# A re-ordered start for an RWKV and gated-MLP kernel: outer products later, half-width down projections earlier, idle matmuls moved

## The chip, the cores and the metric

The program runs on one core of a Trainium2 chip. The metric is the device time of the execution in microseconds; three runs of the kernel before gave 528.74, 527.22 and 528.25 us, median 528.25. The profiled execution took 528.38 us, of which its instructions span 526.6.

## The reference

An RWKV recurrence and then a gated feed-forward layer. For each of 4 batches and 8 heads, over 768 tokens with head size 48 and a state of 48 x 48:

```python
for t in range(S):
    kt, vt, rt = (k[:, :, t], v[:, :, t], r[:, :, t])
    cur = np.einsum('bhd,bhe->bhde', u[None] * kt, vt)
    y[:, :, t] = np.einsum('bhd,bhde->bhe', rt, state + cur)
    state = w[None, :, :, None] * state + np.einsum('bhd,bhe->bhde', kt, vt)
...
x = attn_out.transpose(0, 2, 1, 3).reshape(B * S, H * D)      # 3072 x 384
gate = 1.0 / (1.0 + np.exp(-(x @ w_gate)))                    # 384 x 1536
val = x @ w_val
out = gate * val @ w_out                                      # 1536 x 384
```

All inputs and the output are float32.

## The kernel before, in words

The recurrence is cut into 12 chunks of 64 tokens. A chunk has two groups of heads, so there are 24 groups, numbered in the order (chunk 0, g 1), (chunk 0, g 0), (chunk 1, g 1) and so on. A group's work is: load its channels (`L`) and tokens (`X`); scale queries, keys, bonus keys and token keys by tables of decay powers (`R`, `k`, `A`, `T`); 64 small matmuls for the scores (`Z`, line 392); masked copies of the scores out of PSUM by VectorE (`K`, line 400); the outputs (`I`), which are 32 matmuls from the state, a drain and 32 matmuls from the scores, into two banks of PSUM (line 354); 32 matmuls of outer products for the state (`O`, line 354 too), which go into columns 256 to 447 of the same two banks (for group 1 alone into two banks of their own); decay of the state (`d`) and its update (`s`); and x in two float32r parts, a rounded high part (`h`, ScalarE, line 493) and the low rest (`l`, VectorE, line 497). A fill (`F`) moves leftover rows of x by DMA.

The feed-forward layer works on tiles of two chunks (512 columns) and 12 blocks of 128 hidden units. A block has a gate projection (`u`) and a value projection (`v`) of nine matmuls each (line 531; three parts of x times three pairings of high and low parts: the first two matmuls of a part read the high x, the third the low x), a sigmoid (`g`), a product (`m`), the split of h in a high and a low part (`H`, and `q` on POOL or `qv` on VectorE), and nine down-projection matmuls into three accumulators (`D`, line 573). In the first tile, blocks 0 and 1 are computed in two halves of 256 columns, marked a (chunk 0) and b (chunk 1), since the a half can start before chunk 1 is done. Weights come in as raw words (`W`), from which each block's high and low parts are made by a cast (`c`), a join of words (`j`), a rounding (`w`) and a subtraction (`o`).

`N.k` is k matmuls of bf16 128x512 on a constant, whose result nobody reads (`idle_matmuls`, line 641).

PSUM has a ring of three banks (`one_bank`) for the outputs of groups and the projections, two banks for the scores, and three for the accumulators. A new tile of the ring waits until the readers of the old one are done.

The order of the work up to the end of the first tile is written by hand in the string `START`. Each word is a step and its argument: `u.0b` is the gate projection of block 0, half b. Every engine and SP's DMA queue execute their instructions in the order in which the steps stand there; waits between engines come from what the steps read and write, in that same order. After `START` a loop goes over the blocks of the remaining tiles.

```python
for step in START.split():
    name, _, arg = step.partition(".")
    if name == "D":
        finish(block(arg))
    elif name in moe_steps:
        moe_steps[name](moe_of(block(arg)), block(arg)[2])
    else:
        steps[name](*([int(arg)] if arg else []))
```

Of the kernel before, what the change touches and what calls it, by code (L numbers as in the profile page):

```python
# [19 lines left out]
B, H, S, D = 4, 8, 768, 48  # L20
# [22 lines left out]
START = """  # L43
ta L.0 tov.0 tc tb W.0 ts.0 L.1 ts.1 X.0 tz W.1 tk L.2 X.1 to.1 ti.1 X.2 ti.0 A.0 R.0 W.2 k.0 c0.0
tp tr Z.0 tt A.1 K.0 c0.1 tn k.1 I.0 Rv.1 j0.1 h.0 l.0 Tv.0 Z.1 c.1 j0.0 O.0 A.2 j.1 w0.0 sa.0 N.5
T.2 K.1 F.0 w.1 W.3 Rv.2 I.1 T.1 N.4 k.2 L.3 o0v.0 h.1 L.4 Z.2 w0.1 W.4 O.1 X.3 l.1 o0.1 s.1 u.0a
g.0a K.2 v.0a o.1 m.0a c.2 I.2 O.2 R.3 d.2 j.2 u.1a A.3 N.3 H.0a g.1a k.3 h.2 q.0a s.2 v.1a w.2 l.2
m.1a Z.3 T.3 A.4 H.1a N.4 R.4 K.3 c.3 k.4 I.3 O.3 F.2 L.5 W.8 o.2 D.0a X.4 h.3 L.6 Z.4 W.5 l.3 d.3
W.6 L.7 s.3 X.5 u.0b X.6 g.0b j.3 v.0b c.4 w.3 u.2 j.4 qv.1a m.0b H.0b g.2 v.2 q.0b K.4 w.4 Rv.5
u.1b T.4 A.5 v.1b g.1b m.1b D.0b k.5 H.1b I.4 ov.3 O.4 m.2 A.6 R.6 q.1b Z.5 k.6 L.8 d.4 D.1a W.7 h.4  # L50
o.4 s.4 H.2 D.1b K.5 c.6 l.4 Tv.5 u.3 c.5 g.3 j.6 v.3 j.5 qv.2 I.5 h.5 Z.6 l.5 R.7 L.9 A.7 m.3 X.8
d.5 D.2 ub K.6 H.3 O.5 k.7 s.5 w.5 q.3 u.4 c.8 T.6 ov.5 c.7 g.4 v.4 j.7 w.6 m.4 u.5 ov.6 g.5 v.5 I.6
Y.8 R.8 Z.7 W.9 d.6 O.6 W.10 X.7 w.7 W.11 H.4 s.6 X.9 D.3 j.8 h.6 qv.4 w.8 l.6 D.4 m.5 H.5 F.6 ov.7
qv.5 u.6 c.9 g.6 K.7 v.6 ov.8 m.6 Tv.7 H.6 u.7 qv.6 g.7 k.8 v.7 j.9 m.7 w.9 D.5 o.9 u.8 g.8 H.7 v.8
q.7 c.10 D.6 j.10 m.8 I.7 H.8 Z.8 O.7 d.7 R.9 h.7 w.10 s.7 D.7 b.8 ov.10 u.9 l.7 qv.8 g.9 c.11 v.9
F.7 Y.9 j.11 m.9 D.8 w.11 ov.11 u.10 g.10 H.9 qv.9 v.10 m.10 H.10 u.11 qv.10 g.11 t.8 i.8 v.11 K.8
k.9 m.11 D.9 H.11 t.9 D.10 q.11 b.9 T.9 i.9 T.8
"""


# [869 lines left out]
```

## Time and profile before

| | |
|---|---|
| median of 3 runs | 528.25 us |
| profiled execution, time and span | 528.38 us, 526.6 us |
| PE busy (matmul) | 509.7 us, 5220 matmuls |
| DVE, ACT, POOL busy | 202.6, 186.1, 187.2 us |
| largest part of the chain that ended last | up projections (line 531), 56% |
| mean granted TensorE clock | 0.995 of 2.4 GHz |

PE is TensorE's matmuls and PEld its weight loads, which run beside them. DVE is VectorE, ACT ScalarE, POOL GpSimd, SP the queue that issues the DMAs. All times are from the start of the span. The region that the change touches lies between 22 and 60 us.

### The profile page before, as it was taken

To read this page: it belongs to the slowest core of one execution; us is meant where nothing else is said; L and a number is where in the kernel's file an instruction comes from. 1 tells how busy PE (TensorE), PEld (TensorE's weight loads), DVE (VectorE), ACT (ScalarE), POOL (GpSimd) and SP (SyncE) were. 2 spreads that over 40 slices of the span, in tenths; PEclk is the share of its full clock that TensorE was granted. 3 is DMA by queue.
4 is the path that set the end of the run, shared out by engine and by line. 5 is a ranking of instruction groups with operands and counts; after the bars stand their busy time and mean duration, and the time that the engine had idled before them with its cause. 6 is when DMAs were issued, how large, how long until landed. Compare 5 with 4: busy or idle time off the path is not lost.

```text
span 526.6 us, 11976 instructions
## 1 busy us (share of the span) xinstructions
PE 509.7 (97%) x5220; PEld 421.4 (80%) x5220; DVE 202.6 (38%) x345; ACT 186.1 (35%) x395; POOL 187.2 (36%) x158
## 2 busy tenths in 40 slices
PE   3899999999999999999999999999999999999995
PEld 3689788888888788888888888888888888888884
DVE  7877865545242243242341432431442211111112
ACT  5587864534223134233133332331431221311211
POOL 4454402214545252453452452552352111111120
PEclk9899999999999999999999999999999999999999
DMA  8949654123213030420230420312400000100001
GB/s 318 368 144 421 262 191 167 34 75 96 76 64 88 10 107 4 145 88 19 78 98 12 148 87 1 97 36 72 147 17 2 11 7 14 61 0 1 0 2 65
DMA packets 15579, 47.84 MB, mean 91 GB/s; under 512 B 2368, under 2 KB 4928, under 8 KB 14112
## 3 DMA queue, kind: packets, MB, share of 16 engines
q1 hardware_dynamic: 15376, 46.74, 25.5%
q8 instruction: 43, 0.70, 0.6%
q10 hardware_dynamic: 144, 0.26, 0.1%
q14 instruction: 16, 0.13, 0.1%
HBM read 39.92 MB, written 4.72 MB: 85 GB/s over the span
## 4 chain that ended last, share of the span: by engine, by line
PE 95%; DVE 2%; DMA 1%; issue 1%; ACT 0%; SPq 0%; DVEq 0%; ACTq 0%
PE ring L531 56%; PE acc L573 29%; PE ring L354 7%; PE sc L392 3%; DMA chan<-in_ch 1%; DVE score L400 1%; DVE wf L256 0%; PE acc L641 0%; DVE chan L320 0%; ACT dec L296 0%; DVE sg L586 0%; DVE dec L309 0%; DVE xt L497 0%; DVE toks L324 0%; PE acc L354 0%
## 5 line engine op out<-in xcount | busy, mean ns | idle before, releaser
L531 PE MATMUL ring<-xt,wx 128*128 128x512 f32 (+1 forms) x1332 | 306.5, 384 | 0.0
L531 PEld LDWEIGHTS ring<-xt,wx 128*128 128x128 f32 x1332 | 245.2, 188 | 49.8 <-ACT sg L544 0.3
L557 POOL TENSOR_TENSOR h<-sg,h 128x512 fp32r<-128x512 f32 (+1 forms) x65 | 87.1, 1340 | 252.4 <-ACT h L553 252.4
L573 PE MATMUL acc<-h,wx 128*128 128x512 f32 (+1 forms) x666 | 161.3, 387 | 0.0
L573 PEld LDWEIGHTS acc<-h,wx 128*128 128x128 f32 x666 | 121.2, 188 | 25.0 <-DVE h L557 0.2
L548 DVE TENSOR_TENSOR sg<-ring,sg 128x512 f32<-128x512 f32 (+1 forms) x74 | 50.0, 676 | 235.0 <-PE ring L531 233.5
L544 ACT ACTIVATE sg<-ring 128x512 f32<-128x512 f32 (+1 forms) x74 | 43.2, 584 | 156.3 <-PE ring L531 156.3
L553 ACT CAST h<-sg 128x512 fp32r<-128x512 f32 (+1 forms) x74 | 45.0, 609 | 144.1 <-DVE sg L548 137.8
L309 POOL TENSOR_TENSOR dec<-chan,tabk 128x512 f32<-128x512 f32 x21 | 27.7, 1319 | 14.3 <-PE ring L354 14.0
L497 DVE TENSOR_TENSOR xt<-ring,xt 112x256 fp32r<-112x256 f32 (+1 forms) x52 | 19.9, 418 | 32.6 <-ACT xt L493 32.6
L324 POOL TENSOR_TENSOR toks<-toks,tabn 128x384 f32<-128x384 f32 x19 | 23.7, 1253 | 12.5 <-ACT wx L264 9.5
L330 POOL TENSOR_TENSOR dec<-dec,toks 128x384 f32<-128x384 f32 x16 | 16.3, 1017 | 26.9 <-DMA dec<-in_rt 26.7
L320 DVE TENSOR_TENSOR chan<-chan,tabk 128x512 f32<-128x512 f32 x24 | 24.8, 1034 | 0.6 <-ACT dec L296 0.6
L392 PE MATMUL sc<-dec,chan 48*64 48x64 f32 x768 | 17.2, 231 | 7.7 <-DVE chan L320 7.6
L400 DVE COPY_PREDICATED score<-masks,sc 128x512 f32<-128x512 int32 x32 | 23.9, 748 | 1.9 <-PE sc L392 1.1
L447 ACT ACTIVATE state<-state,pw 112x96 f32<-112x96 f32 x80 | 23.4, 362 | 1.8 <-PE ring L354 1.8
L392 PEld LDWEIGHTS sc<-dec,chan 48*64 48x64 f32 x768 | 14.8, 145 | 8.9 <-POOL dec L309 7.6
L466 DVE TENSOR_TENSOR state<-state,ring 48x192 f32<-48x192 f32 (+1 forms) x52 | 17.9, 350 | 8.1 <-PE ring L354 4.3
L256 DVE SCALAR_TENSOR_TENSOR wf<-wr,top 128x1152 int32<-128x1152 int32 (+1 forms) x13 | 16.8, 1304 | 9.5 <-ACT top L249 6.0
L354 PE MATMUL ring<-score,toks 64*48 64x64 f32 (+1 forms) x768 | 16.6, 223 | 3.7 <-issue 2.3
L493 ACT CAST xt<-ring 112x256 fp32r<-112x256 f32 (+1 forms) x52 | 16.7, 363 | 6.6 <-PE ring L354 6.4
L267 POOL TENSOR_TENSOR wx<-wf,wx 128x1152 fp32r<-128x1152 f32 (+1 forms) x5 | 12.5, 2507 | 18.3 <-ACT wx L264 18.3
(63 smaller groups left out, 254.7 us busy)
## 6 DMA issues: line engine op xcount, KB each, us to landing
wr<-in_wt SPq DMA_DIRECT2D x11, 1152.0 KB, 9.1
chan<-in_ch SPq DMA_DIRECT2D x24, 512.0 KB, 4.3
toks<-in_tk SPq DMA_DIRECT2D x24, 400.0 KB, 4.9
out_y<-wf SPq DMA_DIRECT2D x16, 256.0 KB, 2.3
dec<-in_rt SPq DMA_DIRECT2D x16, 192.0 KB, 2.9
xt<-xt SPq DMA_DIRECT2D x30, 64.0 KB, 2.3
wr<-in_wt SPq DMA_DIRECT2D x2, 576.0 KB, 5.5
xt<-xt SPq DMA_DIRECT2D x12, 32.0 KB, 4.3
```

Source lines behind the costliest of these rows:

```text
L309: eng.tensor_tensor(v4(t[:, 0]), v4(chan[n][:, 0]), bc2(table_of(n)[:, :, ::-1]), ALU.mult)
L320: eng.tensor_tensor(v4(k), v4(k), bc2(table_of(n)), ALU.mult)
L324: eng.tensor_tensor(v4(k), v4(k), bc2(tabn[:, 4 * g : 4 * g + 4]), ALU.mult)
L354: nc.tensor.matmul(to[bank][64 * half : 64 * half + m, cs], lhsT, rhs, start=first, stop=stop, skip_group_check=True,)
L392: nc.tensor.matmul(sc[64 * gm : 64 * gm + 64, be, o : o + C], kk[row, cs : cs + C], rr[row, cs : cs + C], start=True, stop=True,)
L400: nc.vector.copy_predicated(t.rearrange("q (b m i) -> q b m i", b=2, m=4), masks[:, m].bitcast(I32).unsqueeze(1).unsqueeze(1).broadcast_to ...
L531: nc.tensor.matmul(o[:, self.cols], w[a][:, g * DM + kt * P : g * DM + (kt + 1) * P], self.x[:, kt, b, self.cols], start=(k == 0), stop=(k ...
L544: nc.scalar.activation(sg[:, c], self.pair[f][0][:, c], AF.Sigmoid, scale=UP)
L548: nc.vector.tensor_tensor(sg[:, c], self.pair.pop(f)[1][:, c], sg[:, c], ALU.mult)
L553: nc.scalar.copy(out=h[:, 0, c], in_=sg[:, c])
L557: eng.tensor_tensor(h[:, 1, c], self.sg.pop(f)[:, c], h[:, 0, c], ALU.subtract)
L573: nc.tensor.matmul(self.acc[d][:, self.cols], w[a][:, 2 * DM + d * P : 2 * DM + (d + 1) * P], h[:, b, self.cols], start=(f == 0 and k == 0 ...
```

## The change

Only the string `START` changes. Seen by engine, the order changes as follows; everything not named keeps its place.

- PE: `N.4` behind `Z.3` is removed and `N.3` is added behind `v.1a`. `O.2 u.1a N.3 v.1a Z.3 N.4 I.3 O.3 D.0a Z.4 u.0b` becomes `O.2 u.1a N.3 v.1a N.3 Z.3 D.0a I.3 Z.4 D.1a O.3 u.0b`, and `Z.5 D.1a D.1b u.3` becomes `Z.5 D.1b u.3`.
- DVE: `s.2 l.2` becomes `l.2 s.2`; the low part of h of block 1a moves to POOL (`qv.1a` becomes `q.1a`).
- ACT: `d.2 A.3 H.0a g.1a h.2 w.2` becomes `A.3 H.0a h.2 g.1a d.2 w.2`; `c.3 h.3 d.3 g.0b c.4` becomes `h.3 d.3 g.0b c.3 c.4`.
- POOL: `q.0a T.3 R.4 o.2` becomes `q.0a R.4 T.3 q.1a o.2`.
- SP: `L.3 L.4 W.4 X.3` becomes `L.3 X.3 L.4 W.4`.

Between engines, `h.3` now stands before `O.3` in the string and `l.3` still behind it.

```diff
-T.2 K.1 F.0 w.1 W.3 Rv.2 I.1 T.1 N.4 k.2 L.3 o0v.0 h.1 L.4 Z.2 w0.1 W.4 O.1 X.3 l.1 o0.1 s.1 u.0a
-g.0a K.2 v.0a o.1 m.0a c.2 I.2 O.2 R.3 d.2 j.2 u.1a A.3 N.3 H.0a g.1a k.3 h.2 q.0a s.2 v.1a w.2 l.2
-m.1a Z.3 T.3 A.4 H.1a N.4 R.4 K.3 c.3 k.4 I.3 O.3 F.2 L.5 W.8 o.2 D.0a X.4 h.3 L.6 Z.4 W.5 l.3 d.3
-W.6 L.7 s.3 X.5 u.0b X.6 g.0b j.3 v.0b c.4 w.3 u.2 j.4 qv.1a m.0b H.0b g.2 v.2 q.0b K.4 w.4 Rv.5
-u.1b T.4 A.5 v.1b g.1b m.1b D.0b k.5 H.1b I.4 ov.3 O.4 m.2 A.6 R.6 q.1b Z.5 k.6 L.8 d.4 D.1a W.7 h.4
-o.4 s.4 H.2 D.1b K.5 c.6 l.4 Tv.5 u.3 c.5 g.3 j.6 v.3 j.5 qv.2 I.5 h.5 Z.6 l.5 R.7 L.9 A.7 m.3 X.8
...
+T.2 K.1 F.0 w.1 W.3 Rv.2 I.1 T.1 N.4 k.2 L.3 o0v.0 h.1 X.3 Z.2 w0.1 L.4 O.1 W.4 l.1 o0.1 s.1 u.0a
+g.0a K.2 v.0a o.1 m.0a c.2 I.2 O.2 A.3 R.3 H.0a j.2 h.2 u.1a q.0a g.1a k.3 N.3 l.2 d.2 R.4 v.1a s.2
+N.3 T.3 m.1a w.2 Z.3 A.4 H.1a D.0a q.1a K.3 F.2 k.4 L.5 I.3 W.8 X.4 Z.4 L.6 o.2 h.3 W.5 D.1a W.6 O.3
+L.7 d.3 X.5 X.6 l.3 s.3 u.0b g.0b c.3 v.0b j.3 c.4 w.3 j.4 m.0b u.2 H.0b g.2 q.0b K.4 w.4 Rv.5 v.2
+T.4 A.5 u.1b g.1b v.1b m.1b H.1b D.0b k.5 I.4 ov.3 O.4 m.2 A.6 R.6 q.1b Z.5 k.6 L.8 d.4 o.4 D.1b W.7
+h.4 s.4 H.2 K.5 c.6 u.3 l.4 Tv.5 c.5 g.3 j.6 v.3 j.5 I.5 qv.2 h.5 Z.6 l.5 R.7 L.9 A.7 m.3 X.8 d.5
...
```

## Rows read from the trace of the kernel before

**Rows 1.** The page: busy time by engine, and the chain's shares by engine.
```profile
PE 509.7 (97%) x5220; PEld 421.4 (80%) x5220; DVE 202.6 (38%) x345; ACT 186.1 (35%) x395; POOL 187.2 (36%) x158
...
PE 95%; DVE 2%; DMA 1%; issue 1%; ACT 0%; SPq 0%; DVEq 0%; ACTq 0%
```

**Rows 2.** The chain in order of time: start us, us, what, between 26 and 53.
```profile
26.47 0.61 PE ring L354 x27
...
29.77 0.66 PE acc L641 x3
...
31.59 1.14 PE sc L392 x64
...
34.50 1.14 PE ring L354 x59
35.64 1.26 PE acc L573 x9
36.90 1.09 PE sc L392 x64
...
48.40 0.15 issue
...
50.63 2.35 PE acc L573 x18
```

**Rows 3.** DVE's timeline, 31 to 47 us: start, us, instruction, idle before.
```profile
31.03 0.75 DVE L497 TENSOR_TENSOR xt<-ring,xt 112x256 fp32r<-112x256 f32 x2
...
32.75 1.53 DVE L400 COPY_PREDICATED score<-masks,sc 128x512 f32<-128x512 int32 x2 [0.64 <-PE sc L392]
...
36.48 1.73 DVE L497 TENSOR_TENSOR xt<-ring,xt 48x256 fp32r<-48x256 f32 x4 [1.59 <-ACT xt L493]
...
41.37 1.36 DVE L256 SCALAR_TENSOR_TENSOR wf<-wr,top 128x1152 int32<-128x1152 int32 x1 [1.23 <-issue]
42.64 0.42 DVE L557 TENSOR_TENSOR h<-sg,h 128x256 fp32r<-128x256 f32 x1
...
46.85 0.42 DVE L548 TENSOR_TENSOR sg<-ring,sg 128x256 f32<-128x256 f32 x1 [1.45 <-ACT sg L544]
```

**Rows 4.** PE's timeline, 38.43 to 38.66 us: the third matmul of `u.0b` on.
```profile
38.27 0.62 PE L531 MATMUL ring<-xt,wx 128*128 128x256 f32 x3
```

**Rows 5.** The weight loads' timeline (PEld), at the start of `v.1a`.
```profile
30.24 0.90 PEld L531 LDWEIGHTS ring<-xt,wx 128*128 128x128 f32 x7 [0.30 <-ACT sg L544]
```

**Rows 6.** PE's timeline: second part of `I.3`, `O.3`, and the start of `I.4`.
```profile
34.50 0.68 PE L354 MATMUL ring<-score,toks 64*64 64x64 f32 x32 [0.24 <-DVE score L400]
34.99 0.65 PE L354 MATMUL ring<-toks 64*64 64x48 f32 x32
...
47.72 0.68 PE L354 MATMUL ring<-dec,state 48*64 48x64 f32 x32
```

**Rows 7.** ACT's timeline: `h.3`, `g.0b`, `H.0b`, `g.1b`, and `c.6` with `c.5`.
```profile
35.71 1.51 ACT L493 CAST xt<-ring 48x256 fp32r<-48x256 f32 x4 [1.05 <-PE ring L354]
...
39.47 0.38 ACT L544 ACTIVATE sg<-ring 128x256 f32<-128x256 f32 x1 [1.05 <-PE ring L531]
...
43.43 0.41 ACT L553 CAST h<-sg 128x256 fp32r<-128x256 f32 x1 [1.16 <-DVE sg L548]
...
46.46 0.36 ACT L544 ACTIVATE sg<-ring 128x256 f32<-128x256 f32 x1
...
52.98 2.90 ACT L249 ACTIVATE top<-wr 128x1152 f16<-128x1152 bf16 x2 [0.41 <-DMA wr<-in_wt]
```

**Rows 8.** POOL's timeline: `R.6` and `q.1b`.
```profile
48.58 1.71 POOL L309 TENSOR_TENSOR dec<-chan,tabk 128x512 f32<-128x512 f32 x1 [1.39 <-PE ring L354]
50.25 1.19 POOL L557 TENSOR_TENSOR h<-sg,h 128x256 fp32r<-128x256 f32 x1
```

**Rows 9.** Windows: busy us of each engine, then granted clock, DMA share, GB/s.
```profile
16.46:19.88 3.42, 1.53 (x35) 0.80 (x33) 3.39 (x5) 1.47 (x3) 2.50 (x2) 1.00 0.92 293
19.88:23.29 3.41, 3.41 (x66) 1.99 (x64) 2.02 (x5) 2.14 (x5) 0.98 (x1) 0.50 0.89 352
```

More of the change, by code (lines that the diff above doesn't have):

```diff
@@ L51 @@
-o.4 s.4 H.2 D.1b K.5 c.6 l.4 Tv.5 u.3 c.5 g.3 j.6 v.3 j.5 qv.2 I.5 h.5 Z.6 l.5 R.7 L.9 A.7 m.3 X.8
[L52 to L55, printed above, removed]
@@ L56 @@
-F.7 Y.9 j.11 m.9 D.8 w.11 ov.11 u.10 g.10 H.9 qv.9 v.10 m.10 H.10 u.11 qv.10 g.11 t.8 i.8 v.11 K.8
-k.9 m.11 D.9 H.11 t.9 D.10 q.11 b.9 T.9 i.9 T.8
+T.2 K.1 F.0 w.1 W.3 Rv.2 I.1 T.1 N.4 k.2 L.3 o0v.0 h.1 X.3 Z.2 w0.1 L.4 O.1 W.4 l.1 o0.1 s.1 u.0a
+g.0a K.2 v.0a o.1 m.0a c.2 I.2 O.2 A.3 R.3 H.0a j.2 h.2 u.1a q.0a g.1a k.3 N.3 l.2 d.2 R.4 v.1a s.2
+N.3 T.3 m.1a w.2 Z.3 A.4 H.1a D.0a q.1a K.3 F.2 k.4 L.5 I.3 W.8 X.4 Z.4 L.6 o.2 h.3 W.5 D.1a W.6 O.3
+L.7 d.3 X.5 X.6 l.3 s.3 u.0b g.0b c.3 v.0b j.3 c.4 w.3 j.4 m.0b u.2 H.0b g.2 q.0b K.4 w.4 Rv.5 v.2
@@ new lines @@
+T.4 A.5 u.1b g.1b v.1b m.1b H.1b D.0b k.5 I.4 ov.3 O.4 m.2 A.6 R.6 q.1b Z.5 k.6 L.8 d.4 o.4 D.1b W.7
+h.4 s.4 H.2 K.5 c.6 u.3 l.4 Tv.5 c.5 g.3 j.6 v.3 j.5 I.5 qv.2 h.5 Z.6 l.5 R.7 L.9 A.7 m.3 X.8 d.5
+D.2 ub K.6 H.3 O.5 k.7 s.5 w.5 q.3 u.4 c.8 T.6 ov.5 c.7 g.4 v.4 j.7 w.6 m.4 u.5 ov.6 g.5 v.5 I.6 Y.8
+R.8 Z.7 W.9 d.6 O.6 W.10 X.7 w.7 W.11 H.4 s.6 X.9 D.3 j.8 h.6 qv.4 w.8 l.6 D.4 m.5 H.5 F.6 ov.7 qv.5
+u.6 c.9 g.6 K.7 v.6 ov.8 m.6 Tv.7 H.6 u.7 qv.6 g.7 k.8 v.7 j.9 m.7 w.9 D.5 o.9 u.8 g.8 H.7 v.8 q.7
@@ L58 @@
+c.10 D.6 j.10 m.8 I.7 H.8 Z.8 O.7 d.7 R.9 h.7 w.10 s.7 D.7 b.8 ov.10 u.9 l.7 qv.8 g.9 c.11 v.9 F.7
+Y.9 j.11 m.9 D.8 w.11 ov.11 u.10 g.10 H.9 qv.9 v.10 m.10 H.10 u.11 qv.10 g.11 t.8 i.8 v.11 K.8 k.9
+m.11 D.9 H.11 t.9 D.10 q.11 b.9 T.9 i.9 T.8
 """
```

## The prediction

> **What bounds the kernel now.** I read the page's busy times first, then the chain that ended last, then TensorE's (PE's) timeline between 26 and 58 us, where every edit lies. PE is busy for 97% of the span and is 95% of the chain [rows 1]: from about 24 us on, the time is PE's list of work plus the few moments at which that list stops. So an edit of the written order counts only by the PE instructions it adds or removes, and by the stops it makes or fills. Idle time on the other engines costs nothing until PE waits for them.
>
> The stretch that is rewritten stops in one place. After the scores of group 3 (`Z.3`) PE runs four idle matmuls and the state part of `I.3`, and then waits for `K.3` on VectorE (DVE), whose two copies take 1.53 us [rows 2, 3]. From `Z.3`'s end at 32.73 to the second part of `I.3` at 34.50 there are 1.77 us, of which only the part from the state, 0.61 us as at `I.2`, is work [rows 2]. Farther on, `u.0b` runs two matmuls and its third starts at 38.27; the third is the first that reads the low half of x, and `l.3`, which writes it, ends at 36.48 + 1.73 = 38.21 [rows 3, 4]. `u.0b` is thus already tied to `l.3`, with no slack. That is the place to watch.
>
> **The change, part by part.**
>
> *Idle matmuls.* `N.4` behind `Z.3` goes and an `N.3` comes behind `v.1a`. Three take 0.66 us [rows 2]. The `N.3` that stays behind `u.1a` is free: `v.1a` cannot start until ScalarE (ACT) has read `u.1a`'s bank, which is what its weight load waits for [rows 5]. The new one has no such cover: in the trace `Z.3` follows `v.1a` at once, so its inputs were ready. Cost 0.66 us; nothing, if one of the moved inputs of `Z.3` came later by as much.
>
> *`D.0a` between `Z.3` and `I.3`, in `N.4`'s place.* Its nine matmuls took 1.26 us [rows 2]. With the 0.61 us from the state and 0.15 us for the drain behind it (as at `I.4` [rows 2]) that is 2.02 us against the 1.53 us of `K.3`: the wait for the mask copies is covered. The high and low parts of its h are moved ahead on ACT and POOL and are ready near 29.6 us. Of the 1.77 us, 0.61 + 0.15 stay: 1.01 us saved.
>
> *`O.3` behind `Z.4` and `D.1a`; `D.1a` ahead of the second half.* On PE's list this only moves work. From `v.1a`'s end at 31.59 it runs: `N.3` to 32.25, `Z.3` (1.14) to 33.39, `D.0a` to 34.65, state part and drain to 35.41, the scores part of `I.3` to 35.90 (0.49, from its start at 34.50 to that of `O.3` at 34.99), `Z.4` (1.09) to 36.99, `D.1a` (like `D.0a`) to 38.25, `O.3` (0.65) to 38.90 [rows 2, 6]. None of them waits: `q.1a` on POOL ends near 34.8, `k.4` near 35.6, and `h.3` on ACT runs right behind `I.3`, 1.51 us [rows 7], to about 37.6, before `O.3` wants to write the same banks.
>
> But `l.3` reads those banks too, and in the new order it stands behind `O.3`. Group 3's outer products go into columns 256 on of the two banks whose first 256 columns hold its outputs. In the trace `h.3`, which stood behind `O.3`, starts at 35.71 after 1.05 us of waiting for PE [rows 7]; `I.3`'s last matmul had ended by 35.2, `O.3`'s ended at 34.99 + 0.65 = 35.64 [rows 6]. The reader waited for matmuls into other columns. Until now `D.0a` and `Z.4` lay between `O.3` and `u.0b` (1.26 + 1.09 = 2.35 us) and hid most of `h.3` and `l.3`; in the new order nothing lies between. So `l.3` starts at 38.97, the same 0.07 behind `O.3`. Its four copies took 1.73 us in step with `h.3`; two copies in series took 0.75 [rows 3], so at least 1.50. I take 1.50, since `h.3` is long done, and keep 1.73 for the range: end 40.47, `u.0b`'s third matmul at T = 40.53 instead of 38.27. PE idles some 1.3 us before it. A wait of 0.24 us goes and this one is late next. Behind `l.3` on DVE stand `s.3` and `j.3`: `s.3` frees the two banks at about 41.1, before `v.0b` asks near 41.5, and `j.3` has a later bound of its own (below).
>
> The Trainium skill has a rule on this, in "PSUM — Partial Sum Buffer", section "PSUM bank collisions raise a hardware error": accesses of two engines to one bank and 32-partition quadrant must be kept apart by semaphore, by bank and not by address. The row of `h.3` agrees, at one place only; by the rule the wait of `l.3` is certain, and without it the sum would be that of the second rival.
>
> *`c.3` behind `g.0b` on ACT.* Before, `c.3` ran at 33.1 us, in time that ACT had free. Now ACT waits for `u.0b` with nothing to do and then has `c.3` and `c.4` in front of everything else. From rows of before: `g.0b` starts 1.20 us after `u.0b`'s third matmul (39.47 against 38.27) and takes 0.38; two such casts take 2.90, so `c.4` ends at T+4.48; `j.4` on DVE starts 0.09 behind it, the next on DVE 1.27 after that, and this is `m.0b` now, 0.42 long, to T+6.26; `H.0b` 0.03 later; from `H.0b` to `g.1b` ACT is busy without a gap (`H.0b`, `g.2`, `w.4`, `A.5`), 43.43 to 46.46, so `g.1b` at T+9.3, `m.1b` 0.39 behind it for 0.42, to T+10.1 [rows 3, 4, 7]. `I.4` needs two of the three ring banks, those of `u.1b` and `v.1b`, so it cannot start before T+10.1. PE's own list reaches `I.4` at T+9.45 (47.72 less 38.27 [rows 4, 6]). The difference of 0.65 us is a new stop. Below: nothing, if the ring hands `I.4` other banks. Above: 1.2, if `j.3` and `w.3`, each of which needs the one before, don't overlap the casts.
>
> *`D.1b` alone behind `Z.5`.* `D.1a` and `D.1b` took 2.35 us there [rows 2]; `D.1b` alone about 1.26: 1.09 us less. But its last three matmuls read what `q.1b` writes on POOL. `R.6` starts when `I.4`'s state part is done, and `q.1b` behind it ended at 50.25 + 1.19 = 51.44, or 3.72 us after `I.4`'s start at 47.72 [rows 6, 8]. Without `D.1a` in front PE asks for it 3.66 us after that start (2.91 to the end of `Z.5` at 50.63 [rows 2], then six matmuls). Cost 0.1 us; bounds 0 and 0.5, since `R.6` and `q.1b` were slow here (1.71 and 1.19 us).
>
> *What costs nothing.* `X.3` ahead of `L.4` on SP's queue: group 3's tokens land earlier and POOL waits less at `T.3`; `L.4` and `W.4` land about 1 us later, before `R.4`, `A.4` and `c.4` ask. `F.2` is issued about 1.2 us earlier, since `l.2` is, and the transfers behind it with it (`X.6` now waits for `O.3`, to 38.9, and its tokens are read 25 us later). `l.2` before `s.2`, `d.2` behind `g.1a`, `R.4` before `T.3`, `q.1a` on POOL instead of DVE: each stays ahead of its reader by over 1 us; if one didn't, its excess would add to T. The moves of `u.3` and `I.5` change no engine's own order.
>
> *Sum.* `I.4` starts at 40.53 + 10.1 = 50.63 instead of 47.72, 2.91 later; minus 1.09 for `D.1a` already done; plus 0.1. That is +1.9 us against the profiled execution, whose time is 528.38 us for a span of 526.6: 530.3. The median of before, 528.25, lies 0.13 below that execution, so I predict 530.2.
>
> **Rivals.**
>
> *The clock falls back.* Ahead of 19.88 us PE was busy for 1.53 of 3.42 us, and the granted clock of the next 3.41 us is 0.50, which is 1.2 GHz [rows 9]. For it: the new idle of 1.3 us is most of the 1.9 us idle there. Against: dense matmuls stand right before and after it, and it comes alone. Price: 3.41 us at half clock lose 1.7 us of PE's work; the wait at `I.4` (0.65) then hides in it: +1.05, 531.2. In "TensorE: Matmul & The Clock Gate", section "What's actually happening", the Trainium skill says that the throttled state is the default and activity releases it; by that this rival is possible, and it gives no time of its own.
>
> *`l.3` does not wait for `O.3`* (not slower). Then `u.0b` runs on at 38.9, its third matmul at 39.25; `I.4` at 49.35 by ACT's list, or 48.70 if ACT isn't late either: +1.63 or +0.98, less 1.09, plus 0.1 at most: 528.9 or 528.1. For it: only `h.3` shows the dependence, and ACT could have been late there for another reason. Against: ACT's row names PE and no other work. It decides if `l.3` in the new trace starts before `O.3`'s last matmul ends.
>
> *The front saves more than I see*: at most the 1.01 us, with the new idle matmuls hidden too and no new stop: 527.2. Nothing in the trace speaks for it, since `Z.3`'s inputs are ready.
>
> **How the numbers follow.** What this measurement can tell from no change is 0.3%, 1.6 us: faster is below 526.7, slower above 529.8. My forecast has 0.50 (its own range 529.3 to 530.9, about seven tenths of it above 529.8), the clock 0.20, `l.3` not waiting 0.22, the last rival and what I haven't seen 0.08. Slower: 0.35 + 0.20 + 0.02 = 0.57; faster 0.05; the same 0.38. The range runs from 528.0 (just under the second rival) to 531.9 (the clock with the upper bounds of `l.3` and `q.1b`).
>
> **What would show it.** Right: three idle matmuls at 31.5 us directly before `Z.3`; `D.0a` in front of `I.3`, whose wait no longer names DVE's `score`; `l.3` starting right behind `O.3`'s end near 39 us with PE named as releaser; a PE idle of over 1 us inside `u.0b`; one of about 0.6 us before `I.4` that names DVE's or ACT's `sg`; `D.1b` slightly stretched; the clock at 2.4 GHz from 23.3 us on. Wrong: `u.0b` running through without a gap, or its third matmul before 39.5; `I.4` less than 1.1 us later than now; a stretch at 1.2 GHz after 40 us.

## The result, and the profile after

| | before | after |
|---|---|---|
| median | 528.5 us (6 runs, 527.22 to 529.06) | 533.87 us (6 runs, 532.04 to 534.66) |
| profiled execution, time and span | 528.38 us, 526.6 us | 533.94 us, 532.2 us |

The ratio is 1.0101, with an interval of 1.0082 to 1.012: the changed kernel is slower by 5.4 us, where 1.9 was forecast, and 533.87 lies outside the range of 528.0 to 531.9. The sign was right and the size was not.

The busy times on the page of after are almost those of [rows 1]: PE does the same work, 2.2 us longer.

```profile
PE 511.9 (96%) x5219; PEld 423.3 (80%) x5219; DVE 204.7 (38%) x344; ACT 186.4 (35%) x395; POOL 189.4 (36%) x159
```

PE's timeline of after from 30 us on (start us, us, instruction, in brackets the idle time before it and what ended it) answers to [rows 2, 4, 6]:

```profile
30.16 0.82 PE L641 MATMUL acc<-spare 128*128 128x512 bf16 x3
30.91 0.69 PE L392 MATMUL sc<-dec,chan 48*64 48x64 f32 x32
...
32.01 1.33 PE L573 MATMUL acc<-h,wx 128*128 128x256 f32 x9
...
34.19 0.68 PE L354 MATMUL ring<-score,toks 64*64 64x64 f32 x32 [0.24 <-issue]
36.70 0.69 PE L392 MATMUL sc<-dec,chan 48*64 48x64 f32 x32 [1.83 <-DVE chan L320]
...
37.80 1.70 PE L573 MATMUL acc<-h,wx 128*128 128x256 f32 x9
39.43 1.09 PE L354 MATMUL ring<-toks 64*64 64x48 f32 x32
40.45 0.79 PE L531 MATMUL ring<-xt,wx 128*128 128x256 f32 x2
42.45 9.73 PE L531 MATMUL ring<-xt,wx 128*128 128x256 f32 x52 [1.21 <-DVE xt L497]
...
53.19 0.79 PE L354 MATMUL ring<-dec,state 48*64 48x64 f32 x32
...
57.46 0.62 PE L573 MATMUL acc<-h,wx 128*128 128x256 f32 x3 [0.35 <-POOL h L557]
57.91 0.40 PE L531 MATMUL ring<-xt,wx 128*128 128x512 f32 x1
```

From top to bottom: the three idle matmuls directly before `Z.3`; `D.0a` behind it; `I.3`'s scores part, which waits no longer for VectorE; then `Z.4`, which stops for 1.83 us until `k.4` (line 320) is done; `D.1a` and `O.3`, which take 1.63 and 1.02 us from start to start where the forecast had 1.26 and 0.65 (from 38.56 on the clock is at half, as the windows below show); the foreseen stop of `u.0b` for `l.3`; and the stop of `D.1b`.

The timelines of the other engines, of after, show what stands behind those stops:

```profile
33.58 2.87 DVE L320 TENSOR_TENSOR chan<-chan,tabk 128x512 f32<-128x512 f32 x1
40.67 1.73 DVE L497 TENSOR_TENSOR xt<-ring,xt 48x256 fp32r<-48x256 f32 x4 [4.22 <-PE ring L354]
...
53.76 1.35 DVE L267 TENSOR_TENSOR wx<-wf,wx 128x1152 fp32r<-128x1152 f32 x1
...
55.63 1.18 DVE L320 TENSOR_TENSOR chan<-chan,tabk 128x512 f32<-128x512 f32 x1
...
32.58 0.74 POOL L557 TENSOR_TENSOR h<-sg,h 128x256 fp32r<-128x256 f32 x1 [1.06 <-ACT h L553]
33.28 2.62 POOL L267 TENSOR_TENSOR wx<-wf,wx 128x1152 fp32r<-128x1152 f32 x1
...
54.15 2.11 POOL L309 TENSOR_TENSOR dec<-chan,tabk 128x512 f32<-128x512 f32 x1 [2.49 <-issue]
56.22 1.19 POOL L557 TENSOR_TENSOR h<-sg,h 128x256 fp32r<-128x256 f32 x1
...
44.41 0.38 ACT L544 ACTIVATE sg<-ring 128x256 f32<-128x256 f32 x1 [6.76 <-PE ring L531]
44.69 2.89 ACT L249 ACTIVATE top<-wr 128x1152 f16<-128x1152 bf16 x2
```

`k.4` takes 2.87 us, and on POOL `o.2` (line 267) begins 0.30 us before it and lasts until 35.90. In the kernel before the same two instructions met the other way round: `k.4` began 0.15 us before `o.2`, and was done in 0.73 us (timelines of DVE and of POOL, before):

```profile
34.16 0.73 DVE L320 TENSOR_TENSOR chan<-chan,tabk 128x512 f32<-128x512 f32 x1
...
34.31 3.10 POOL L267 TENSOR_TENSOR wx<-wf,wx 128x1152 fp32r<-128x1152 f32 x1
```

Whoever starts first runs at its own pace and the other one waits: before, `o.2` was 0.48 us longer than in after; in after, `k.4` ends 0.55 us behind `o.2`, as if it had begun when `o.2` ended. The Trainium skill states it so, in "SBUF — State Buffer", section "SBUF: two separate sides": a VectorE operation with two SBUF inputs and a GpSimd operation that reads SBUF take turns on a shared pair of ports, and the first to start holds it for its whole instruction. Both rows agree.

The windows of after (start:end, length, busy us of PE, PEld, DVE, ACT and POOL, granted clock, DMA share, GB/s) show the second loss:

```profile
35.14:38.56 3.42, 1.85 (x70) 1.82 (x71) 1.31 (x1) 2.44 (x8) 0.76 (x1) 1.00 0.94 343
38.56:45.39 6.83, 5.62 (x52) 5.01 (x52) 2.31 (x6) 0.98 (x2) 0.00 (x0) 0.50 1.02 423
45.39:52.00 6.61, 6.61 (x40) 5.87 (x40) 5.65 (x6) 5.96 (x9) 1.71 (x2) 1.00 0.84 344
```

After the stop at `Z.4` the granted clock is 0.50, which is 1.2 GHz, for 6.83 us.

In these two profiled executions the start of `v.1a` to that of `u.3` lasted 22.58 us before and 28.93 after, 6.35 more. The front up to `v.1a` was 1.26 us shorter in this execution, mostly because the stretch at half clock of [rows 9] isn't in it, and the part behind `u.3` 0.5 longer: together the 5.56 between the two times.

### The profile page after: what moved, and what is told of

Its sections match the earlier page's. It is cut to its first block, busy times and chain, and to the rows that moved or that the text cites. A ratio compares the mean times of both kernels' runs of the same rounds, so it can differ in the third digit from the quotient of the medians.

```text
span 532.2 us, 11969 instructions
## 1 busy us (share of the span) xinstructions
PE 511.9 (96%) x5219; PEld 423.3 (80%) x5219; DVE 204.7 (38%) x344; ACT 186.4 (35%) x395; POOL 189.4 (36%) x159
## 4 chain that ended last, share of the span: by engine, by line
PE 90%; issue 1%; POOL 0%; DVE 0%; DVEq 0%
PE ring L531 55%; PE acc L573 28%; PE ring L354 5%; PE sc L392 2%; POOL h L557 0%; DVE sg L586 0%; DVE xt L497 0%; PE ring L221 0%; POOL dec L309 0%; DVEq L586 0%
## 5 line engine op out<-in xcount | busy, mean ns | idle before, releaser
L557 POOL TENSOR_TENSOR h<-sg,h 128x512 fp32r<-128x512 f32 (+1 forms) x66 | 88.2, 1336 | 259.6 <-ACT h L553 259.6
L324 POOL TENSOR_TENSOR toks<-toks,tabn 128x384 f32<-128x384 f32 x19 | 24.9, 1313 | 9.6 <-ACT wx L264 9.6
L320 DVE TENSOR_TENSOR chan<-chan,tabk 128x512 f32<-128x512 f32 x24 | 27.1, 1131 | 1.2 <-ACT dec L296 1.2
L249 ACT ACTIVATE top<-wr 128x1152 f16<-128x1152 bf16 (+1 forms) x13 | 18.1, 1423 | 0.4 <-DMA wr<-in_wt 0.4
```

What stands on the lines that cost most here:

```text
L320: eng.tensor_tensor(v4(k), v4(k), bc2(table_of(n)), ALU.mult)
L324: eng.tensor_tensor(v4(k), v4(k), bc2(tabn[:, 4 * g : 4 * g + 4]), ALU.mult)
L557: eng.tensor_tensor(h[:, 1, c], self.sg.pop(f)[:, c], h[:, 0, c], ALU.subtract)
```

## The experiments

Two theories for the 3.5 us beyond the forecast (5.4 less 1.9). In the expectations, A says that it all begins at `Z.4`: `o.2` holds `k.4`, PE stands still for 1.83 us, and the clock falls for that. The rival, B, says that the clock falls for another reason, the stop for `l.3` or the data that now moves there, and takes its part whatever `Z.4` does. Each kernel starts from after, if nothing else is said. Before's own median in the three batches of runs was 529.26, 529.03 and 529.2 us (18 to 30 runs each): e1 to e4 in the first, e5 to e8 in the second, e9 and e10 in the third, the first on another chip than the rest. Ratios are against it.

**e1: `o.2` on VectorE, behind `k.4`.**

```diff
-K.3 F.2 k.4 L.5 I.3 W.8 X.4 Z.4 L.6 o.2 h.3
+K.3 F.2 k.4 L.5 I.3 W.8 X.4 Z.4 L.6 ov.2 h.3
```

> Changed kernel, but the subtraction o.2 (the low weights of block 2) runs on VectorE behind k.4 instead of on POOL beside it. Theory A (k.4 was held up by POOL's o.2, and that stop of 1.83 us ahead of Z.4 is what brought the clock down): k.4 takes 0.7 us instead of 2.87, Z.4 follows I.3 without a stop, the clock stays at 2.4 GHz, u.0b still stops about 1.2 us for l.3, and the time is about 530.3, my forecast's sum (529.6 to 531). Theory B (the stop inside u.0b alone is enough for the clock): k.4 is short but a stretch at 1.2 GHz still follows u.0b's stop, time about 531.5 to 532.5.

Measured: 530.6 us (12 runs), ratio 1.0035 [1.0016, 1.0054], or +1.9 us. DVE's and then PE's timeline of e1:

```profile
33.86 0.68 DVE L320 TENSOR_TENSOR chan<-chan,tabk 128x512 f32<-128x512 f32 x1
...
35.07 0.66 PE L392 MATMUL sc<-dec,chan 48*64 48x64 f32 x32
...
39.99 8.57 PE L531 MATMUL ring<-xt,wx 128*128 128x256 f32 x52 [1.50 <-DVE xt L497]
...
49.57 1.13 PE L354 MATMUL ring<-dec,state 48*64 48x64 f32 x32
```

`k.4` takes 0.68 us, `Z.4` doesn't stop, and the clock, in the same window as above, stays up although the stop for `l.3` is there with 1.50 us:

```profile
38.56:45.39 6.83, 5.39 (x31) 4.83 (x32) 4.28 (x8) 4.10 (x4) 0.00 (x0) 1.00 1.01 414
```

One instruction on another engine takes back 3.3 us between the medians, and what is left, 1.9 us, is the size of the forecast's sum. From `Z.3` to `u.3` the two profiled executions differ by 3.58 us (27.00 in after; 31.22 to 54.64, so 23.42, here): 1.94 of it lies between `Z.3` and `Z.4`, the other 1.64 behind, where after's clock is at half.

**e2: after, with eight idle matmuls in front of `Z.4`**, so that PE doesn't stand still while `k.4` is held.

```diff
-I.3 W.8 X.4 Z.4
+I.3 W.8 X.4 M.8 Z.4
...
+    def idle_in_ring(k):
+        t, bits = one_bank(), ident.bitcast(BF16)
+        for _ in range(k):
+            nc.tensor.matmul(
...
+        "N": idle_matmuls, "M": idle_in_ring,
```

> Changed kernel with eight idle matmuls (bf16 128x512, into a free bank of the ring) between I.3 and Z.4, 1.8 us of them, in the time in which PE waited for k.4. Both theories: k.4 still takes about 2.9 us beside o.2, and no stop of PE is left before Z.4. Theory A: the clock stays at 2.4 GHz through 38 to 45 us, so that only the stops themselves are left: about 1.8 for k.4 and 1.2 for l.3 on top of the forecast's other terms, 531.5 to 532.3, some 1.5 to 2.4 below the changed kernel. Theory B: a stretch at 1.2 GHz follows the stop in u.0b all the same, time within 0.8 of the changed kernel (533 to 534.5).

Measured: 534.25 us (6 runs), ratio 1.0091 [1.0056, 1.0127]; A's number is missed, and the time lies in B's range. PE's timeline and a window of e2:

```profile
35.86 1.90 PE L649 MATMUL ring<-spare 128*128 128x512 bf16 x8
...
42.73 0.62 PE L531 MATMUL ring<-xt,wx 128*128 128x256 f32 x3 [1.50 <-DVE xt L497]
44.21 9.62 PE L531 MATMUL ring<-xt,wx 128*128 128x256 f32 x49 [0.87 <-issue]
```

```profile
45.26:48.68 3.42, 3.42 (x13) 2.93 (x12) 1.77 (x2) 3.30 (x4) 0.00 (x0) 0.50 1.02 429
```

The stop at `Z.4` is filled, and the clock stays full up to 45.26. But a new stop of 0.87 us, "issue", comes behind that of `l.3`, and after the two the clock falls all the same, for 3.42 us. So the run doesn't tell what the clock alone is worth: A keeps the `k.4` part (e1), B is right that a fall can follow the stop for `l.3` too.

**e9: `k.4` ahead of `K.3`**, with `o.2` left on POOL, to see whether the order alone decides.

```diff
-q.1a K.3 F.2 k.4 L.5 I.3
+q.1a k.4 K.3 F.2 L.5 I.3
```

> Changed kernel with one word moved: k.4 ahead of K.3 on VectorE, so that it starts near 32.2 us, before POOL's o.2 does (33.3). Theory A (whichever of the two starts first runs, the other waits for it): k.4 takes 0.7 to 1.0 us, o.2 its 2.6, Z.4 follows I.3 without a stop, and the time is that of e1, 530.6 (530 to 531.2), although o.2 stays on POOL. Rival (e1 gained because POOL had less to do, or because o.2 came sooner): the stop ahead of Z.4 stays, 532.5 to 534.

Measured: 531.41 us (7 runs), ratio 1.0042 [1.0027, 1.0057]. Timelines of DVE, POOL and PE in e9:

```profile
34.70 0.69 DVE L320 TENSOR_TENSOR chan<-chan,tabk 128x512 f32<-128x512 f32 x1 [1.46 <-ACT dec L296]
...
35.95 2.63 POOL L267 TENSOR_TENSOR wx<-wf,wx 128x1152 fp32r<-128x1152 f32 x1
...
37.39 0.65 PE L392 MATMUL sc<-dec,chan 48*64 48x64 f32 x32
```

The same instructions on the same engines, `k.4` 1.25 us ahead of `o.2`: 0.69 instead of 2.87 us, no stop at `Z.4`, 2.5 us gained. It is the order of the two, not their number. The 0.2 us above the expected range stay open.

**e3: `l.3` ahead of `O.3`**, `o.2` left on POOL.

```diff
-D.1a W.6 O.3 L.7 d.3 X.5 X.6 l.3 s.3 u.0b
+D.1a W.6 l.3 O.3 L.7 d.3 X.5 X.6 s.3 u.0b
```

> Changed kernel with l.3 ahead of O.3 in the order (PE's own order is the same). Theory A's second half (l.3 waited for O.3 because the two touch the same bank): l.3 starts right behind h.3 and k.4 near 36.5 us, u.0b runs through without a stop. The stop before Z.4 stays (k.4 about 2.9 us) and with it one stretch at 1.2 GHz, now 3.4 us long instead of 6.8: time about 531.3 (530.5 to 532.2). Rival (l.3 was late for another reason): l.3 ends where it ended, u.0b stops as before, 533 to 534.7.

Measured: 534.01 us (6 runs), ratio 1.0082 [1.005, 1.0113]: a miss, no gain in the median. PE's timeline of e3, and a window:

```profile
38.01 0.69 PE L392 MATMUL sc<-dec,chan 48*64 48x64 f32 x32 [1.55 <-DVE chan L320]
...
40.96 1.70 PE L531 MATMUL ring<-xt,wx 128*128 128x256 f32 x12
44.52 7.14 PE L531 MATMUL ring<-xt,wx 128*128 128x256 f32 x42 [1.85 <-issue]
```

```profile
37.00:42.00 5.00, 3.99 (x113) 3.77 (x114) 2.98 (x7) 2.19 (x7) 0.21 (x1) 1.00 1.00 363
```

The stop for `l.3` is gone, and three matmuls into `v.0b` PE stops for 1.85 us and waits for nothing that the profile names. Counting all PE instructions of the trace by their start (matmuls, weight loads, semaphore waits, drains), the stop lies before the 1474th, and so do those of 0.87 us in e2 and 0.29 us in e6 (the expectations count from zero: 1473rd). "issue" stops of PE in the front lie before the 450th and the 706th, all a multiple of 256 apart, and the page lists 43 packets on an instruction queue, 0.70 MB, that is 16 KB each. In the records of that queue a block begins to arrive at 42.02, 5.9 us after PE has begun the instruction one block ahead, the 1218th, at 36.12; in before, where the loads stand later, 1.3 us after it (34.95 and 36.22). Theory C: the block of instructions stands behind the data.

In the two profiled executions the stretch from `Z.3` to `u.3` is 2.3 us shorter in e3 than in after (32.20 to 56.86, so 24.66, against 27.00), and no fall of the clock follows the stop at `Z.4`; the front of e3 is 1.3 us longer, with a stretch at half clock of its own. Why the medians show none of this stays open.

**e5: e3, with five loads behind `X.6`.**

```diff
-L.5 I.3 W.8 X.4 Z.4 L.6 o.2 h.3 W.5 D.1a W.6 l.3 O.3 L.7 d.3 X.5 X.6 s.3
+L.5 I.3 X.4 Z.4 o.2 h.3 D.1a l.3 O.3 d.3 X.5 X.6 L.6 W.5 W.6 L.7 W.8 s.3
```

> As e3 (l.3 ahead of O.3, k.4 still beside POOL's o.2), but the five large loads L.6, W.5, W.6, L.7 and W.8 are issued only behind X.6, which waits for O.3. In e3 PE stopped for 1.85 us inside v.0b, at its 1473rd instruction, with no engine to wait for; the instruction queue's 16 KB transfer had started at 42.0, some 4 us behind the instruction that seems to ask for it, while data moved at 370 to 440 GB/s. Theory C (PE waited for its own instructions, whose transfer stood behind data): with the loads later that transfer starts within 1.5 us, the stop inside v.0b is gone, time 1.5 to 2 below e3: 531.8 to 532.6. Rival (the stop has another cause, such as a bank or the fill of x): it stays, 533.5 to 534.5.

Measured: 532.76 us (7 runs), ratio 1.007 [1.0045, 1.0095]. The median is 1.25 us below that of e3, but the two intervals overlap, so it is the trace that decides. PE's timeline of e5, and the window that answers to e3's:

```profile
37.69 0.69 PE L392 MATMUL sc<-dec,chan 48*64 48x64 f32 x32 [1.84 <-DMA chan<-in_ch]
...
40.65 8.88 PE L531 MATMUL ring<-xt,wx 128*128 128x256 f32 x54
```

```profile
37.00:42.00 5.00, 4.31 (x116) 4.09 (x117) 2.65 (x7) 1.59 (x6) 0.00 (x0) 1.00 0.65 215
```

With 215 instead of 363 GB/s the block begins to arrive 2.0 us after the 1218th instruction (35.51 and 37.51), and all 54 matmuls run through. That PE waited for its instructions is well borne out: at the 1474th it goes on 2.3 to 2.8 us after the block begins to arrive, in e2, e3, e6 and e10 alike (e3's 42.02 is 5.9 us behind the 1218th, not the "some 4" of the expectation). That data in front of the block made it late is borne out by e3 against e5, but it is not the whole: e1, e4 and e6 issue the loads in the same order as after, and there the block comes 2.3, 2.8 and 3.3 us after the 1218th, against 5.8, 6.2 and 5.9 in after, e2 and e3. What else decides is open; e1, e4 and e6 have `o.2` on VectorE. The time gains less than the 1.5 to 2 us expected, because e3's stop had covered others: in e5 the state part of `I.4` takes 1.13 us (0.68 in e3), and `D.1b` stops for 0.35 us (not in e3).

The stop at `Z.4` is still there; DVE has `k.4` at 2.88 us again, although the row names a DMA. No fall of the clock follows it in this execution.

**e4: e1 and e3 together** (`o.2` on VectorE, `l.3` ahead of `O.3`).

```diff
-Z.4 L.6 o.2 h.3 W.5 D.1a W.6 O.3 L.7 d.3 X.5 X.6 l.3 s.3 u.0b
+Z.4 L.6 ov.2 h.3 W.5 D.1a W.6 l.3 O.3 L.7 d.3 X.5 X.6 s.3 u.0b
```

> Changed kernel with both edits: o.2 on VectorE, and l.3 ahead of O.3. Theory A: neither Z.4 nor u.0b stops, the clock stays at 2.4 GHz, and what is left is the front's 0.35 us gained, the stop before I.4 of about 0.6 us that ACT's order with c.3 behind g.0b makes, and 0.1 to 0.35 for q.1b: 528.7 to 529.3, the same as before within 0.3%. Theory B gives the same here. If it is over 530.5, a third cost is missing from both.

Measured: 529.76 us (12 runs), ratio 1.0015 [0.9994, 1.0037], just above the expected range. The median is 0.8 us below that of e1; the intervals overlap. PE's timeline of e4:

```profile
38.67 0.66 PE L354 MATMUL ring<-toks 64*64 64x48 f32 x30 [0.21 <-DVE xt L497]
39.26 8.82 PE L531 MATMUL ring<-xt,wx 128*128 128x256 f32 x54
...
49.09 1.13 PE L354 MATMUL ring<-dec,state 48*64 48x64 f32 x32
...
53.69 0.62 PE L573 MATMUL acc<-h,wx 128*128 128x256 f32 x3 [0.34 <-POOL h L557]
```

`u.0b` runs through, and now `O.3` waits for `l.3`, 0.21 us. `I.4`'s state part takes 1.13 us instead of 0.68 [rows 6], and `D.1b` stops.

**e6: e4, with `c.3` ahead of `h.3` again.**

```diff
-ov.2 h.3 W.5 D.1a W.6 l.3 O.3 L.7 d.3 X.5 X.6 s.3 u.0b g.0b c.3 v.0b
+ov.2 c.3 h.3 W.5 D.1a W.6 l.3 O.3 L.7 d.3 X.5 X.6 s.3 u.0b g.0b v.0b
```

> As e4 (o.2 on VectorE, l.3 ahead of O.3), with the cast c.3 back in front of h.3 on ScalarE. My forecast's step: with c.3 behind g.0b, m.1b is late and I.4 stops about 0.65 us (0.45 in e4's trace, inside its state part). If so, the state part of I.4 runs without the stop and the time is 0.4 to 0.7 below e4: 528.9 to 529.4. Rival (I.4 doesn't wait for that, or q.1b then takes its place): within 0.2 of e4.

Measured: 528.96 us (12 runs), ratio 1.0 [0.9982, 1.0018], as expected; the median is 0.8 us below that of e4, and again the intervals overlap. PE's timeline of e6:

```profile
49.17 0.68 PE L354 MATMUL ring<-dec,state 48*64 48x64 f32 x32
...
52.01 1.51 PE L573 MATMUL acc<-h,wx 128*128 128x256 f32 x9
```

Both losses are gone at once, 1.13 - 0.68 = 0.45 and 0.34 us: the late `c.3` was behind the two.

**e7: before, with the idle edit alone; e8: e6 without its new idle matmuls.**

```diff
-v.1a w.2 l.2 m.1a Z.3 T.3 A.4 H.1a N.4 R.4 K.3
+v.1a N.3 w.2 l.2 m.1a Z.3 T.3 A.4 H.1a R.4 K.3
```

```diff
-v.1a s.2 N.3 T.3 m.1a w.2 Z.3
+v.1a s.2 T.3 m.1a w.2 Z.3
```

> Kernel before with the idle matmuls' edit alone: N.4 behind Z.3 removed, N.3 added behind v.1a. My forecast's terms: the new N.3 has no cover and costs 0.66 us; without D.0a behind Z.3 the wait for K.3 keeps its length whether N.4 fills it or not, so nothing comes back: 0.66 above before, 528.9 to 530. Rival (removing N.4 lets the clock fall in the wait for K.3): 1.5 to 2.5 above before.

> As e6 without the added N.3 behind v.1a. By the forecast's terms PE's list is then 0.66 us shorter: 0.5 to 0.8 below e6, and below the kernel before by about 0.5 to 1 us, if the clock holds without the idle matmuls. Rival (that N.3 keeps the clock up): a stretch at 1.2 GHz after 32 us, 1 us or more above e6.

Measured: e7 529.72 us (12 runs), 1.0011 [0.9991, 1.0031]; e8 528.63 us (12 runs), 0.9999 [0.9976, 1.0023], 0.33 below e6. Both have the sign of the forecast's 0.66, but neither is resolved from zero, and e8's expected 0.5 to 0.8 below e6 is missed. In e7 `k.4` took 2.47 us, with `o.2` begun 0.74 us before it: the idle matmuls' edit alone turns the two around. There `D.0a` still stands ahead of `Z.4`, which stops for 0.17 us only. e8 holds all that the rewrite was to save and none of its three late places, and it only equals before. PE's timeline of e8 shows where most of the saving goes:

```profile
32.27 0.68 PE L354 MATMUL ring<-dec,state 48*64 48x64 f32 x32
33.18 0.84 PE L354 MATMUL ring<-score,toks 64*64 64x64 f32 x32 [0.24 <-issue]
33.94 0.69 PE L392 MATMUL sc<-dec,chan 48*64 48x64 f32 x32
...
36.30 1.01 PE L354 MATMUL ring<-toks 64*64 64x48 f32 x32
37.24 8.68 PE L531 MATMUL ring<-xt,wx 128*128 128x256 f32 x54
```

From start to start, the state part and the drain of `I.3` take 0.91 us (0.76 in the forecast), its scores part 0.76 (0.49), `O.3` 0.94 (0.65): 0.71 us more in all, against the 1.01 saved, in this one execution. Of the 0.29 for `O.3`, 0.2 are a wait of the weight loads for `l.3` (line 497), which now stands before it: the price of that order. For the other two no releaser is named.

**e10: e8, with the loads moved as in e5.**

```diff
-L.5 I.3 W.8 X.4 Z.4 L.6 ov.2 c.3 h.3 W.5 D.1a W.6 l.3 O.3 L.7 d.3 X.5 X.6 s.3
+L.5 I.3 X.4 Z.4 ov.2 c.3 h.3 D.1a l.3 O.3 d.3 X.5 X.6 L.6 W.5 W.6 L.7 W.8 s.3
```

> As e8 (o.2 on VectorE, l.3 ahead of O.3, c.3 early, no N.3 behind v.1a), with the five large loads behind X.6 as in e5. In e8 and e6 PE came to its 1473rd instruction at about the time when its instructions had landed (a stop of 0 to 0.3 us), so the loads' place matters little here: within 0.3 us of e8, and against the kernel before 0 to 1 us faster. Rival (late loads now come too late for c.5, c.6 or Z.6): 0.5 us or more slower than e8.

Measured: 529.24 us (12 runs), 1.0001 [0.9984, 1.0019]. Moving the loads gains nothing here that can be measured, and no version came out measurably below before.

## Why the prediction was wrong

- **The step that failed** stands in the part on `O.3` behind `Z.4`: "None of them waits: `q.1a` on POOL ends near 34.8, `k.4` near 35.6". It took `k.4` at its 0.73 us and asked only whether its inputs come in time. By the forecast's own times `o.2` starts on POOL when `q.1a` ends, at 34.8, and `k.4` when `K.3` is done, near 34.9: the two were on top of each other, and nothing had been asked about that. In its place the runs show `k.4` held for 2.87 us behind `o.2`, a stop of 1.83 us at `Z.4` that the sum doesn't have, and in the profiled execution half clock behind it. With `k.4` free the stop is gone and 3.3 us (e1) or 2.5 us (e9) come back.
- It could have been read from before: `q.1a` on POOL and `R.4` before `T.3` stand under "What costs nothing", judged by their own readers alone, and not by when they let `o.2` begin (2.79 us after `Z.3`'s start in before, 2.37 in after, while `k.4` begins 2.64 and 2.67 us after it); and the row that groups line 320 in before has a spread (ns: least, median, most) that no property of its own explains, for one shape:

```profile
L320 DVE TENSOR_TENSOR chan<-chan,tabk x24: 671/966/1483, 6.6 to 394.6; 128x512 f32<-128x512 f32 x24
```

- **The clock.** The rival named the right loss in the wrong place: it was priced behind the stop of `u.0b`, at 1.7 us, and stands behind that of `Z.4`. After minus e1 gives 1.94 us for the stop and 1.64 for what lies behind it, in one execution each. That the stop brings the fall is not shown: in e5 the same stop, 1.84 us, is followed by full clock, in e1 the stop of `u.0b` alone, 1.50 us, brings no fall, and in e2 one comes after it. Of after's six runs five have a mean granted clock of 0.990 to 0.993 (the profiled one 0.992) and one 0.997; this one took 532.82 us, 2.2 above e1's median, which hints at the stop as the larger part, but a run at 0.993 took 532.04. No run separates the two cleanly.
- **Right: `l.3` behind `O.3`.** In after it starts at 40.67, 0.15 us behind `O.3`'s end, with PE named; the stop in e1 is 1.50 us. The rule that the forecast took from the Trainium skill ("PSUM — Partial Sum Buffer", section "PSUM bank collisions raise a hardware error": to guard by bank, not by address) is how this program waits, in both directions: with `l.3` ahead PE has no stop in `u.0b` (e3, e4), and `O.3` waits for `l.3` (e4). `l.3` took 1.73 us, the upper bound, not the 1.50 of the sum. The forecast's +1.9 is what the medians of e1 and before give, but that is in part luck: in the profiled executions the stretch from `v.1a` to `u.3` is 25.34 us in e1 against 22.58 in before, 2.76 more.
- **Right: `c.3` behind `g.0b`**, forecast 0.65 at `I.4`, measured 0.45 within its state part. In after itself the wait vanishes in the slow stretch, as the rival said.
- **Too small: `q.1b`**, 0.1 forecast, 0.35 measured, inside its bounds. The forecast saw that `R.6` and `q.1b` were slow in before and not why. By the rows of after it is the same taking of turns: `ov.3` (VectorE, line 267, to 55.11), `R.6` (POOL, to 56.26), `k.6` (VectorE, to 56.81) and `q.1b` (POOL, to 57.41) overlap and end 1.15, 0.55 and 0.60 us one after the other, each a little less than such an operation takes alone there (1.29, 0.68 and 0.74). With `c.3` early `ov.3` comes sooner, `R.6` takes 1.68 us and the stop is gone (e6).
- **Right in sign, unresolved in size: `N.3`** (0.66; the medians of e7 and e8 give 0.7 and 0.3). **Too large: `D.0a`'s 1.01**, as e8 shows, and the 1.09 for `D.1b` alone: the two halves took 2.26 us in before from start to start and `D.1b` alone 1.36 in e6, 0.90 less.
- **"What costs nothing"** held for the loads in after only because a longer stop covers them: the instruction block is late there too (it begins to arrive at 40.30), and costs 1.85 us in e3, where `l.3`'s stop is taken away. In e4, with the same loads, it arrives at 38.47 and costs nothing.

Open: the 0.5 us behind `u.3`, how the 3.3 us split between the stop and the clock and why the clock falls, what besides the loads delays the block of instructions, and the 0.8 us between e9 and e1.

## What to carry to other kernels

When an order is rewritten, lay the new times of the engines beside each other, and for each VectorE operation on a path ask what GpSimd has begun just before it: here 0.15 us of lead on one side or 0.30 on the other decided over 2.1 us of `k.4`. Take away one stop and look for the one that it covered, above all where loads were moved forward with the rest. And a stop that was filled gave back less than its length here (e8).

## What was not expected of the hardware

- A VectorE product of 128x512 float32 takes 0.68 to 0.73 us alone, and 2.87, 2.90 and 2.88 us when a POOL subtraction of 2.62 us began 0.27 to 0.30 us before it (after, e3, e5). Each time it ended 0.55 us behind the subtraction.
- PE's instructions come in blocks over a queue of their own, among the data. In e3, with data at 363 GB/s, a block came 5.9 us after the instruction one block ahead and PE stood still for 1.85 us; in e5, at 215 GB/s, it came after 2.0 us and PE did not stop. The stop has no releaser and lies at the same count of PE's instructions in e2, e3, e6 and e10, which is how it can be told from a wait.
- The granted clock fell after a stop of 1.83 us (after) and after stops of 1.50 and 0.87 us close together (e2), and not after stops of 1.84 us (e5), of 1.55 and 1.85 us (e3) or of 1.50 us (e1). In the front it fell after stops of 0.53 and 1.37 us (before) and not after 1.35 and 0.92 us (e7). These executions give no rule for it.
